# Smaller first layer-norm groups, an earlier modulation weight, 2 KB value runs and a new instruction order in a one-core adaLN transformer block

## The chip, the cores and the metric

The kernel runs on one core of a Trainium2 chip. The metric is the device time of one execution in microseconds (us), as the median of several executions. The profile lists the core's instructions by engine (in the kernel before 2264 matmuls on PE, 301 instructions on DVE, 189 on ACT, 81 on POOL): TensorE (PE, with its weight loads as PEld), VectorE (DVE), ScalarE (ACT), GpSimd (POOL) and SyncE (SP). In this kernel SP does nothing but issue DMAs, in a fixed order, each behind the semaphores that it waits for.

## The reference

One transformer block on x of 2048 tokens by 512, bf16, with a modulation from a condition vector c. Cut to what matters:

```python
mod = silu(c) @ w_mod                      # 6 vectors of 512: sa, ca, ga, sb, cb, gb
h = layernorm(x) * (1 + ca) + sa
q, k, v = h @ wqkv                         # 32 heads of 16
# each position attends to 8 keys: itself and those 2, 4, ... 14 positions before
attn = softmax(mask(q . k * 16**-0.5))
x = x + ga * ((attn . v) @ wo)
h = layernorm(x) * (1 + cb) + sb
x = x + gb * ((silu(h @ w1) * (h @ w3)) @ w2)      # w1, w3: 512 x 1792
```

w_mod is 512 x 3072. The kernel loads it in four parts: the first slice of 1 MB holds sa and ca, the second slice of 1 MB holds sb and cb, and two parts of 0.5 MB hold the gates ga and gb.

## The kernel before

x is cut into 16 tiles of 128 tokens. For a group of tiles the kernel normalizes (xn), transposes on TensorE, and applies the modulation while it evicts the result (h, by ScalarE) from PSUM (pall in the profile, which all matmuls here write). Then come the projections q, k and v. The window attention runs as one big VectorE product per tile (pq = q times the eight shifted copies of k, 128x4096), reduced on TensorE; v goes to a DRAM scratch and comes back in another layout (vsh), is multiplied with the weights by a second 128x4096 product and reduced on TensorE.

The program lists its operations with a number for each; a list scheduler at build time picks, for each engine, the ready operation with the lowest number, using modelled costs. So the order of instructions, the DMA order on SP included, comes from a table of numbers that was tuned offline, from the modelled DMA rate and from the pools of buffers.

```python
DMA_RATE = 320
BLOCKS = [[[0]], [[1]], [[2], [3]], [[4, 5], [6, 7]], ...]           # tiles whose exps are one block
LATE = {"wms1": 0, "wmg1": 1, "w13_0": 0, "w13_1": 1, ...}           # these loads wait for a pq product
...
p.dma(... c, transposed, elements of 2 bytes ..., ("load", 0), 1024, w=[vcT])
for T in range(4):
    p.dma(x_sb[:, T, :], x_view[:, T, :], ("load", 1), 131072, w=[vx[T]])
p.dma(wm_s[0][:], wm_view[:, :, 0:1024], ("load", 2), 1048576, w=[vwms[0]])      # first slice of w_mod
... wq, wk, wv, the other x, the first gate's weights, wo ...
late["wms1"] = [p.dma(wm_s[1][:], wm_view[:, :, 1536:2560], ("load", 12), 1048576, ...)]   # second slice
...
# one value tile back from the scratch: one DMA, runs of 8 rows = 8 KB
p.dma(lambda: vv.at[:].rearrange("p g d -> p (g d)"),
      bass.AP(v_dram, (PAD + T * P) * D, [[8 * D, 16], [-DIL * D, W], [1, 8 * D]]), ("vl", T), 1048576, ...)
...
for cch in range(NCH):                                   # four groups of four tiles
    vns = [ln_stats(0, 4 * cch + i) for i in range(4)]
    vh = ln_T(0, cch, vns)
    proj_qk(cch, 0, vh)
    proj_qk(cch, 1, vh)
    for i in range(4):
        proj_v(4 * cch + i, vh)
```

The softmax here doesn't subtract the row's maximum and nothing guards it: scores larger than these inputs give would overflow.

## Time and profile before

| | before |
|---|---|
| time, three runs at the start | 262.87 us (262.56 to 263.39) |
| profiled execution | span 259.8 us |
| TensorE busy | 242.0 us, 93% |
| VectorE busy | 191.5 us, 74% |
| first projection starts | 13.81 us |
| second slice of w_mod, issue to landing | 17.8 us |

From the profile's page: busy time of each engine, the busy tenths of TensorE and its granted clock in 40 slices of the span, the chain of work that ended last, and two of the DMA groups (count, size of each, median us from issue to landing).

```profile
span 259.8 us, 5381 instructions
PE 242.0 (93%) x2264; PEld 138.2 (53%) x2264; DVE 191.5 (74%) x301; ACT 109.1 (42%) x189; POOL 36.8 (14%) x81
...
PE   0489997699999999999999999999999999999995
...
PEclk9999999799999999999999999999999999999999
...
PE 83%; DMA 9%; DVE 4%; ACT 1%; POOL 1%; SPq 1%; issue 0%
...
sb_vsh<-v_scratch_dram SPq DMA_DIRECT2D x13, 1024.0 KB, 8.1
...
sb_wm_s<-in_w_mod_dram SPq DMA_DIRECT2D x2, 1024.0 KB, 11.9
```

The kernel is bound by TensorE: the chain lies on it for 83% of the span. A gain must come from its idle stretches, which are at slices 1 to 3 and at slices 7 and 8, or from the clock, which falls in slice 8 as well. The waits view of TensorE says what it waited for (total us, times, longest):

```profile
PE pall L574 <- DVE sb_xn L558: 6.6, 3, 6.0
PE pall L520 <- DMA sb_wm_s<-in_w_mod_dram: 4.9, 2, 3.7
PE pall L600 <- ACT sb_h L582: 3.1, 1, 3.1
PE pall L660 <- DVE sb_pq L651: 0.2, 1, 0.2
```

The timeline of TensorE shows where (start, us, engine, line, what, count, and in brackets the idle time before it and what ended it):

```profile
6.00 1.14 PE L574 MATMUL pall<-sb_ident,sb_xn 128*128 128x128 bf16 x8 [6.00 <-DVE sb_xn L558]
...
9.26 0.99 PE L520 MATMUL pall<-sb_csT_bf,sb_wm_s 128*128 128x1 bf16 x32 [1.22 <-DMA sb_wm_s<-in_w_mod_dram]
...
13.81 6.07 PE L600 MATMUL pall<-sb_h,sb_wqkv 128*128 128x512 bf16 x20 [3.11 <-ACT sb_h L582]
...
47.59 0.98 PE L520 MATMUL pall<-sb_csT_bf,sb_wm_s 128*128 128x1 bf16 x32 [3.70 <-DMA sb_wm_s<-in_w_mod_dram]
48.43 1.87 PE L600 MATMUL pall<-sb_h,sb_wqkv 128*128 128x512 bf16 x4
...
50.52 2.22 PE L600 MATMUL pall<-sb_h,sb_wqkv 128*128 128x512 bf16 x8
```

There are two costs. At the start, TensorE waits for the first xn, for w_mod and then for four 512-wide evictions of h. At 47.59 us it waits for the second slice of w_mod; the four matmuls after that wait take 1.87 us, where four take 1.03 us elsewhere: the clock was at half speed. The records of the clock show half speed from 47.75 to 51.17 us. They begin only at 17.03 us, with full speed; that the clock was at half before is read from the matmuls, since 20 of them take 6.07 us at 13.81 us where eight take 1.89 us later.

Lastly, the DMA view of the window from 27 to 50 us (GB/s in 40 slices of the window, then two groups):

```profile
GB/s 228 52 82 315 383 383 385 363 347 376 392 185 214 228 214 271 228 199 228 256 228 185 214 271 228 164 178 199 239 338 381 385 367 358 353 347 345 353 373 371
...
sb_vsh<-v_scratch_dram SPq DMA_DIRECT2D x2, 1024.0 KB, 13.9
...
sb_wm_s<-in_w_mod_dram SPq DMA_DIRECT2D x1, 1024.0 KB, 17.8
```

The stretch at about 200 GB/s, from the twelfth figure on, is the two value tiles on their way back. They landed at 40.19 and 44.85 us, behind 1.5 MB of weights, and the slice at 47.45 us behind them.

### The profile page before, as it was taken

How to read it: one execution, taken by the hardware profiler on the slowest of the kernel's cores; microseconds unless marked ns; L12 is line 12 of the kernel's file. 1: busy time of each engine (PE TensorE's matmuls, PEld its weight loads, DVE VectorE, ACT ScalarE, POOL GpSimd, SP SyncE). 2: the span in 40 equal slices, each digit the busy share in tenths (PEclk: the TensorE clock that was granted, in tenths of full speed). 3: DMA queues.
4: the chain of work that ended last, by engine and by line, in shares of the span. 5: the costliest groups of instructions: out<-in, count | busy, mean ns of one | idle time of the engine just before them, and what ended most of it. 6: DMA issues, size and time to landing. Idle time of an engine off the chain costs nothing.

```text
span 259.8 us, 5381 instructions
## 1 busy us (share of the span) xinstructions
PE 242.0 (93%) x2264; PEld 138.2 (53%) x2264; DVE 191.5 (74%) x301; ACT 109.1 (42%) x189; POOL 36.8 (14%) x81
## 2 busy tenths in 40 slices
PE   0489997699999999999999999999999999999995
PEld 0235655356459865656555455455654444566662
DVE  5596999589899998999899869877957434333152
ACT  2347755178677321636474044342205334311210
POOL 6174034100430004000000300001322000000000
PEclk9999999799999999999999999999999999999999
DMA  5992899989989559930784943909200000001001
GB/s 156 361 334 64 260 246 256 357 215 346 241 182 183 136 126 235 213 76 3 182 185 101 222 99 77 191 23 238 67 23 20 1 3 0 20 23 40 20 20 40
DMA packets 38904, 36.27 MB, mean 140 GB/s; under 512 B 18640, under 2 KB 35808, under 8 KB 36832
## 3 DMA queue, kind: packets, MB, share of 16 engines
q1 hardware_dynamic: 38880, 35.94, 54.9%
q8 instruction: 17, 0.28, 0.5%
q14 instruction: 7, 0.06, 0.1%
HBM read 30.67 MB, written 5.26 MB: 138 GB/s over the span
## 4 chain that ended last, share of the span: by engine, by line
PE 83%; DMA 9%; DVE 4%; ACT 1%; POOL 1%; SPq 1%; issue 0%
PE pall L756 37%; PE pall L777 19%; DMA sb_wm_s<-in_w_mod_dram 9%; PE pall L600 8%; PE pall L740 5%; PE pall L727 5%; PE pall L660 3%; PE pall L620 3%; PE pall L574 2%; DVE sb_pq L651 2%; ACT sb_h L582 1%; POOL sb_rs L555 1%; SPq L133 1%; PE pall L520 1%; DVE sb_st L550 0%
## 5 line engine op out<-in xcount | busy, mean ns | idle before, releaser
L756 PE MATMUL pall<-sb_h,sb_w 128*128 128x512 bf16 (+1 forms) x560 | 101.0, 336 | 0.0
L756 PEld LDWEIGHTS pall<-sb_h,sb_w 128*128 128x128 bf16 x560 | 53.9, 98 | 41.3
L762 ACT ACTIVATE sb_sg<-pall 128x512 bf16<-128x512 f32 (+1 forms) x70 | 35.4, 512 | 69.1 <-PE pall L756 69.0
L765 DVE TENSOR_TENSOR sb_hh<-sb_sg,pall 128x512 bf16<-128x512 bf16 (+1 forms) x70 | 38.6, 577 | 25.4 <-PE pall L756 21.8
L777 PE MATMUL pall<-sb_w,sb_hh 128*128 128x512 bf16 x224 | 51.3, 379 | 0.0
L651 DVE TENSOR_TENSOR sb_pq<-sb_q,sb_kT 128x4096 bf16<-128x4096 bf16 x16 | 36.3, 2282 | 2.3 <-ACT sb_q L607 1.9
L553 POOL TENSOR_TENSOR sb_rs<-sb_mv,sb_cst 128x1 f32<-128x1 f32 x32 | 14.3, 446 | 160.3 <-DVE sb_mv L551 160.1
L600 PE MATMUL pall<-sb_h,sb_wqkv 128*128 128x512 bf16 x128 | 33.1, 404 | 3.1 <-ACT sb_h L582 3.1
L777 PEld LDWEIGHTS pall<-sb_w,sb_hh 128*128 128x128 bf16 x224 | 21.5, 98 | 23.1
L718 DVE TENSOR_TENSOR sb_vsh<-sb_vsh,sb_al 128x4096 bf16<-128x4096 bf16 x13 | 29.6, 2285 | 3.2 <-DMA sb_al<-a_scratch_dram 2.2
L582 ACT ACTIVATE sb_h<-pall,sb_modc 128x512 bf16<-128x512 bf16 (+1 forms) x36 | 23.8, 730 | 18.9 <-PE pall L574 13.8
L550 DVE BATCH_NORM_STATS2 sb_st<-sb_x 128x6 f32<-128x512 bf16 x32 | 21.7, 679 | 3.2 <-DMA sb_x<-in_A_x_dram 2.9
L783 DVE TENSOR_TENSOR sb_o<-pall,sb_x 128x512 bf16<-128x512 f32 x16 | 11.0, 690 | 17.4 <-PE pall L777 17.2
L600 PEld LDWEIGHTS pall<-sb_h,sb_wqkv 128*128 128x128 bf16 x128 | 12.5, 103 | 17.1 <-ACT sb_h L582 3.4
L555 POOL TENSOR_TENSOR sb_rs<-sb_rs,sb_cst 128x1 f32<-128x1 f32 x32 | 20.4, 637 | 2.5
L574 PE MATMUL pall<-sb_ident,sb_xn 128*128 128x128 bf16 x128 | 12.6, 233 | 6.6 <-DVE sb_xn L558 6.6
L733 ACT ACTIVATE sb_ot<-pall 128x512 bf16<-128x512 f32 x16 | 9.6, 598 | 21.8 <-PE pall L727 19.8
L660 PEld LDWEIGHTS pall<-sb_E,sb_pq 128*128 128x128 bf16 x512 | 15.0, 96 | 3.2 <-ACT sb_h L582 0.3
L740 PE MATMUL pall<-sb_wo,sb_ot 128*128 128x512 bf16 x64 | 15.9, 379 | 0.0
L620 PE MATMUL pall<-sb_wqkv,sb_h 128*128 128x512 bf16 x64 | 15.8, 379 | 0.0
L574 PEld LDWEIGHTS pall<-sb_ident,sb_xn 128*128 128x128 bf16 x128 | 9.2, 103 | 12.0 <-DVE sb_xn L558 7.9
L660 PE MATMUL pall<-sb_E,sb_pq 128*128 128x32 bf16 x512 | 15.3, 176 | 0.2 <-DVE sb_pq L651 0.2
(59 smaller groups left out, 156.9 us busy)
## 6 DMA issues: line engine op xcount, KB each, us to landing
sb_vsh<-v_scratch_dram SPq DMA_DIRECT2D x13, 1024.0 KB, 8.1
sb_vshx<-v_scratch_dram SPq DMA_DIRECT2D x3, 1024.0 KB, 7.1
sb_wm_s<-in_w_mod_dram SPq DMA_DIRECT2D x2, 1024.0 KB, 11.9
v_scratch_dram<-sb_v SPq DMA_DIRECT2D x16, 128.0 KB, 6.3
sb_w<-in_B_w_dram SPq DMA_DIRECT2D x4, 512.0 KB, 11.9
out_dram<-sb_o SPq DMA_DIRECT2D x16, 128.0 KB, 1.7
sb_w<-in_B_w_dram SPq DMA_DIRECT2D x1, 1792.0 KB, 8.8
sb_wqkv<-in_A_wqkv_dram SPq DMA_DIRECT2D x3, 512.0 KB, 8.7
```

What stands on the lines that cost most here:

```text
L574: ins = e.transpose(b[:, col:col + P], vns[tt].at[:, ft * P:(ft + 1) * P], ident[:])
L582: return e.activation(vh.at[:, ft, 0:n * P], b[:, j * 512:j * 512 + n * P], ACT.Identity, bias=modc[:, 8 * which + ft:8 * which + ft + 1], ...
L600: ins = e.matmul(bank(vp), wqkv[:, t, col:col + P], vh.at[:, t, :], start=(t == 0), stop=(t == KT - 1))
L620: ins = e.matmul(bank(vp), vh.at[:, t, tt * P:(tt + 1) * P], wqkv[:, t, 2 * D:3 * D], start=(t == 0), stop=(t == KT - 1))
L651: return e.tensor_tensor(vp.at[:], in0, in1, ALU.mult)
L660: ins = e.matmul(b[:, c0:c0 + H], vp.at[:, w, ft, :], E_sb[:, ft, :], start=(ft == 0), stop=(ft == KT - 1))
L718: return e.tensor_tensor(v_w, v_w, a_w, ALU.mult)
L740: ins = e.matmul(bank(vy), vt.at[:, ft, :], wo[:, ft, :], start=(ft == 0), stop=(ft == KT - 1))
L756: ins = e.matmul(bank(vp)[:, 0:n], wt[:, t, fi * P:(fi + 1) * P], vh.at[:, t, 0:n], start=(t == 0), stop=(t == KT - 1))
L762: p.op("act", lambda e: e.activation(vt.at[:, 0:n], bank(vgp)[:, 0:n], ACT.Silu), c_act(n), k, r=[vgp], w=[vt], table="silu")
L765: p.op("dve", lambda e: e.tensor_tensor(vh_.at[:, 0:n], vt.at[:, 0:n], bank(vup)[:, 0:n], ALU.mult), c_dve(n), k, r=[vt, vup], w=[vh_])
L777: ins = e.matmul(bank(vz), vhh[fi].at[:, tt * P:(tt + 1) * P], w2[:, fi, :], start=(fi == 0), stop=(fi == NF - 1))
```

## The change

The intent is to start TensorE's projections sooner, and to keep the second modulation from ever waiting. In parts:

1. The first two layer-norm groups have two tiles rather than four, so the first evictions of h are 256 wide, and half of them go to VectorE. c is loaded from ACT's queue; two x tiles go ahead of w_mod and two behind it.
2. The second slice of w_mod stands ahead of all FFN weights on SP.
3. A value tile comes back as four DMAs with runs of 2 KB, not as one with runs of 8 KB.
4. The exps are blocked per pair of tiles, and all the numbers are tuned anew, so the order of instructions differs on every engine.

```diff
-DMA_RATE = 320
+DMA_RATE = 350
-BLOCKS = [[[0]], [[1]], [[2], [3]], [[4, 5], [6, 7]], [[8, 9], [10, 11]], [[12, 13], [14, 15]]]
-LATE = {"wms1": 0, "wmg1": 1, "w13_0": 0, "w13_1": 1, "w13_2": 2, "w13_3": 3, "w2": 4}
+BLOCKS = [[[0]], [[1]], [[2, 3]], [[4, 5]], [[6, 7]], [[8, 9]], [[10, 11]], [[12, 13], [14, 15]]]
+VG = 2
+LN1 = [[0, 1], [2, 3], [4, 5, 6, 7], [8, 9, 10, 11], [12, 13, 14, 15]]
+LATE = {"wms1": 0, "wmg1": 2, "w13_0": 0, "w13_1": 1, "w13_2": 1, "w13_3": 2, "w2": 2}
@@ loads
-    p.dma(... c ..., ("load", 0), 1024, w=[vcT])
+    p.dma(... c ..., ("load", 0), 1024, w=[vcT], eng="act")
     for T in range(4):
-        p.dma(x_sb[:, T, :], x_view[:, T, :], ("load", 1), 131072, w=[vx[T]])
+        p.dma(x_sb[:, T, :], x_view[:, T, :], ("load", 1 if T < 2 else 19), 131072, w=[vx[T]])
@@ evictions of h
+                if half and not which and gi < 2:
+                    p.op("dve", ev_dve, c_dve(n * P), k, r=[vt, vmod[which]], part=[vh])
+                else:
+                    p.op("act", ev, c_act(n * P) + 150, k, r=[vt, vmod[which]], part=[vh])
@@ value tile
+        for g in range(0, 8, VG):
+            p.dma(lambda g=g: vv.at[:, g:g + VG, :].rearrange("p g d -> p (g d)"),
+                  bass.AP(v_dram, (PAD + T * P + g) * D, [[8 * D, 16], [-DIL * D, W], [1, VG * D]]), ("vl", T), VG * 131072, ...)
@@ groups
-    for cch in range(NCH):
-        vns = [ln_stats(0, 4 * cch + i) for i in range(4)]
+    for gi, Ts in enumerate(LN1):
+        vns = [ln_stats(0, T) for T in Ts]
... the tables of numbers, projections of n columns, and one small VectorE operation less per modulation: left out ...
```

## The prediction

> **What bounds the kernel now.** TensorE. The engine table has PE busy 242.0 of a 259.8 us span (93%), DVE 191.5 (74%). PE's warm durations (0.216 us for a 512-column matmul, 0.109 for 256, 0.79 per logits or value reduction) add up to about 237 us. In the timeline PE's first projection starts at 13.81 us, after waits for xn (6.0), w_mod's DMA (1.2) and h (3.1); one more wait, 3.70 us ending at 47.59, is for the second w_mod slice, which took 17.85 us to land behind FFN weights and V loads. After that PE never idles over 0.3 us until 256.8; the tail is 3.0 us. Half-speed matmuls cost about 1.6 us before 17.0 (20 projections in 6.07 us, not 4.3) and 1.7 us after the 3.7 us gap (granted clock 0.5 for 3.4 us)[...].
>
> **What the change does.**
> 1. Start. w_mod is issued third, at about 1.7 us instead of 3.13, and c's 2-byte descriptors, during which almost no data moved (about 1.3 us), leave SP's queue for ACT's. w_mod lands near 7 instead of 9.12. The first h needs two tiles; its four evictions are 256 wide, two on ACT, two on DVE: about 0.9 us instead of 2.79. First projection at about 10.0; with 0.2 us less PE work before it, **gain 3.6 us**.
> 2. Second w_mod slice. It goes ahead of all FFN weights; only V loads (2 MB) precede it. I estimate landing at 33-36 us; PE wants it at about 36. The wait and its half-speed window go: **gain 5.0 us**.
> 3. V loads. Today's 8 KB packets move 110-115 KB per 0.5 us, where 1 and 2 KB packets move 165-185. With 2 KB runs a load should take 3-4 us rather than 4.2-4.7. V loads are not on PE's chain; this protects step 2. Cost: 48 more issues of 0.55 us on SP, hidden.
> 4. Exp per pair: two more table loads (1.28 us each) on ACT, 42% busy: nothing. 256-column projections: PE time the same within 0.1 us.
> 5. **New cost:** PE's work comes 8-9 us earlier while DVE's keeps its size. Adding DVE durations in the new order leaves only 1-2 us of slack ahead of PE's reductions between 27 and 85 us, and the first attention reloads queue behind 3.5 MB of FFN weights. I charge **1.5 us** of small PE waits.
>
> **Sum.** 262.9 - 3.6 - 5.0 + 1.5 = 255.8; I say **255.6 us**, range 252.8 to 259.6. Nothing shortens PE's 237 us, so about 252.5 is the floor. Chances: faster by over 2% (under 257.6) 0.78, within 2% 0.19, slower 0.03.
>
> **What the profile would show.** Step 1: first projection at 9.5-10.8 us. Step 2: no PE wait for w_mod over 1 us, no 0.5 clock window after 20 us. Step 3: V loads faster per MB, no PE wait for them. Step 5: PE waits on DVE products between 27 and 85 us, 1-3 us in all; DVE over 95% busy there, its total within 2 us of 191.
>
> **What would make it wrong.** c's tiny descriptors beside x may delay x and w_mod, halving step 1. The q/k weights now come after v and x; past 13.5 us PE waits and cools again. If 2 KB V runs are no faster, or SP blocks behind a V store, the second slice is late again (up to 4 us back). If DVE cannot hold the tighter plan, PE waits of 3-5 us appear before 90 us: 258-259.

## The result, and the profile after

| | before | after |
|---|---|---|
| time, same rounds | 263.13 us (4 runs, 262.56 to 264.07) | 255.37 us (4 runs, 254.32 to 255.82) |
| ratio | | 0.9696, 95% interval 0.9651 to 0.9741 |
| profiled span | 259.8 us | 253.2 us |
| first projection starts | 13.81 us | 10.51 us |
| second slice lands | 47.45 us | 36.90 us |

A ratio here is the mean time of one kernel's fast runs over that of the other's of the same rounds, so it is not quite the ratio of the quoted medians. Later, on chip 12, the changed kernel was run again (label after_again): 255.08 us against 262.20, ratio 0.9719 (0.9686 to 0.9751). All outputs are right.

From the page of the changed kernel:

```profile
span 253.2 us, 5473 instructions
PE 239.0 (94%) x2262; PEld 140.4 (55%) x2296; DVE 191.7 (76%) x298; ACT 111.4 (44%) x198; POOL 32.0 (13%) x81
...
PE   0599989999999999999999999999999999999995
...
PEclk9999999999999999999999999999999999999999
...
PE 87%; DVE 5%; DMA 2%; POOL 2%; issue 1%; SPq 0%; ACT 0%; DVEq 0%
...
sb_vsh<-v_scratch_dram SPq DMA_DIRECT2D x48, 256.0 KB, 4.4
...
sb_wm_s<-in_w_mod_dram SPq DMA_DIRECT2D x2, 1024.0 KB, 6.6
```

DMA's share of the chain fell from 9% to 2%, and no slice of the clock is below 9. The waits of TensorE:

```profile
PE pall L574 <- DVE sb_xn L558: 6.4, 2, 5.6
PE pall L522 <- DMA sb_wm_s<-in_w_mod_dram: 1.5, 1, 1.5
PE pall L633 <- DVE sb_xn L558: 1.3, 1, 1.3
PE pall L633 <- ACT sb_q L622: 0.2, 1, 0.2
```

One wait for w_mod is left, the one at the start. Its timeline:

```profile
5.62 0.61 PE L574 MATMUL pall<-sb_ident,sb_xn 128*128 128x128 bf16 x4 [5.62 <-DVE sb_xn L558]
7.76 0.99 PE L522 MATMUL pall<-sb_csT_bf,sb_wm_s 128*128 128x1 bf16 x32 [1.54 <-DMA sb_wm_s<-in_w_mod_dram]
...
10.51 3.59 PE L633 MATMUL pall<-sb_wqkv,sb_h 128*128 128x512 bf16 x8 [1.30 <-DVE sb_xn L558]
...
37.56 0.29 PE L574 MATMUL pall<-sb_ident,sb_xn 128*128 128x128 bf16 x2 [0.75 <-DVE sb_xn L558]
...
39.34 0.94 PE L522 MATMUL pall<-sb_csT_bf,sb_wm_s 128*128 128x1 bf16 x32
```

The wait of 1.30 us at 10.51 is put down to xn, which came last by the semaphores, but it is the time of the evictions of h: two on ScalarE and two on VectorE, between 9.4 and 10.5 us. The second modulation at 39.34 has no wait before it at all. The eight matmuls at 10.51 take 3.59 us, nearly twice what eight take at full speed (1.89): TensorE starts its projections at half clock here as well, and the records show full clock only from 16.28 us.

The mean granted clock of every run (an average over the execution, in which the half speed of the start isn't counted) shows the late half-speed stretch without a profile. One stretch of 3.41 us at half speed is a loss of 1.7 us of 260, so it makes 0.993, and two make 0.987. Of the 31 runs of the kernel before made beside the experiments, 11 had 0.992 or 0.993 and 20 had 0.985 to 0.987; none had 1.0. All ten runs of the changed kernel had 1.0.

### The profile page after: what moved, and what is told of

Same layout as the page of the kernel before. It is cut to its first block, busy times and chain, and to the rows that moved or that the text cites. A ratio compares the mean times of both kernels' runs of the same rounds, so it can differ in the third digit from the quotient of the medians.

```text
span 253.2 us, 5473 instructions
## 1 busy us (share of the span) xinstructions
PE 239.0 (94%) x2262; PEld 140.4 (55%) x2296; DVE 191.7 (76%) x298; ACT 111.4 (44%) x198; POOL 32.0 (13%) x81
## 4 chain that ended last, share of the span: by engine, by line
PE 87%; DVE 5%; DMA 2%; POOL 2%; issue 1%; SPq 0%; ACT 0%; DVEq 0%
PE pall L771 36%; PE pall L792 19%; PE pall L615 9%; PE pall L755 5%; PE pall L742 5%; PE pall L633 5%; PE pall L673 4%; PE pall L574 2%; DMA sb_x<-in_A_x_dram 2%; POOL sb_rs L555 1%; DVE sb_xn L558 1%; DVE sb_st L550 1%; POOL sb_rs L553 1%; DVE sb_pq L664 1%; DVE sb_hh L780 1%
## 5 line engine op out<-in xcount | busy, mean ns | idle before, releaser
L771 PE MATMUL pall<-sb_h,sb_w 128*128 128x512 bf16 (+1 forms) x548 | 100.0, 336 | 0.7
L780 DVE TENSOR_TENSOR sb_hh<-sb_sg,pall 128x512 bf16<-128x512 bf16 (+1 forms) x70 | 39.5, 577 | 26.0 <-PE pall L771 23.8
L792 PE MATMUL pall<-sb_w,sb_hh 128*128 128x512 bf16 x216 | 49.7, 379 | 0.4
L615 PE MATMUL pall<-sb_h,sb_wqkv 128*128 128x512 bf16 (+1 forms) x155 | 31.9, 344 | 0.3
L582 ACT ACTIVATE sb_h<-pall,sb_modc 128x512 bf16<-128x512 bf16 (+1 forms) x36 | 23.1, 708 | 18.7 <-PE pall L574 13.1
L553 POOL TENSOR_TENSOR sb_rs<-sb_mv,sb_cst 128x1 f32<-128x1 f32 x32 | 8.8, 276 | 151.4 <-DVE sb_mv L551 148.4
L733 DVE TENSOR_TENSOR sb_vsh<-sb_vsh,sb_al 128x4096 bf16<-128x4096 bf16 x12 | 27.3, 2285 | 0.4 <-DMA sb_vsh<-v_scratch_dram 0.4
L615 PEld LDWEIGHTS pall<-sb_h,sb_wqkv 128*128 128x128 bf16 x160 | 15.1, 101 | 11.0 <-ACT sb_h L582 0.7
L633 PE MATMUL pall<-sb_wqkv,sb_h 128*128 128x512 bf16 x63 | 17.6, 411 | 1.5 <-DVE sb_xn L558 1.3
L574 PEld LDWEIGHTS pall<-sb_ident,sb_xn 128*128 128x128 bf16 x128 | 9.5, 101 | 10.6 <-DVE sb_xn L558 6.9
L755 PE MATMUL pall<-sb_wo,sb_ot 128*128 128x512 bf16 x58 | 15.0, 379 | 0.3
```

The source lines that it names most:

```text
L574: ins = e.transpose(b[:, col:col + P], vns[tt].at[:, ft * P:(ft + 1) * P], ident[:])
L615: ins = e.matmul(bank(vp)[:, 0:n], wqkv[:, t, col:col + P], vh.at[:, t, 0:n], start=(t == 0), stop=(t == KT - 1))
L633: ins = e.matmul(bank(vp), vh.at[:, t, tt * P:(tt + 1) * P], wqkv[:, t, 2 * D:3 * D], start=(t == 0), stop=(t == KT - 1))
L733: return e.tensor_tensor(v_w, v_w, a_w, ALU.mult)
L755: ins = e.matmul(bank(vy), vt.at[:, ft, :], wo[:, ft, :], start=(ft == 0), stop=(ft == KT - 1))
L771: ins = e.matmul(bank(vp)[:, 0:n], wt[:, t, fi * P:(fi + 1) * P], vh.at[:, t, 0:n], start=(t == 0), stop=(t == KT - 1))
```

## Where the time went, from the two traces

In the profiled executions, over the 6.6 us of span:

| TensorE, us | before | after | difference |
|---|---|---|---|
| waits before the first projection (6.00+0.29+1.22+3.11; 5.62+1.54+1.30) | 10.6 | 8.5 | -2.2 |
| lost to half clock at the start (half of the busy time until full clock, modulation left out: 5.5; 7.0) | 2.8 | 3.5 | +0.7 |
| wait for the second slice | 3.7 | 0 | -3.7 |
| lost to half clock after that wait (half of 2.7, modulation left out) | 1.4 | 0 | -1.4 |
| other waits of at least 0.2 us (0.24+0.28; 0.20+0.75) | 0.5 | 1.0 | +0.4 |
| sum | | | -6.2 |

The modulation's 32 one-column matmuls are left out of the half-clock rows because the clock hardly changes them: they took 0.99 us at half speed (9.26 us, before) and 0.94 us at full speed (39.34 us, after). The 0.4 us that the sum leaves over stays unassigned; idle times under 0.2 us are not counted, and some matmul records are missing (the page of the changed kernel counts 2262 matmuls and 2296 weight loads).

The profiled execution of before was one of its faster ones (261.81 us against a median of 263.13), with one late half-speed stretch.

## The experiments

The experiments keep the compiled order of one of the two kernels and change one thing. `_move` takes operations out of the scheduled list and puts them behind another; the order on the other engines stays, and the semaphores are worked out anew. The theory was: the gain is the earlier start plus the absent wait for the second slice with its half-speed stretch, and the rest of the change is worth little. The rivals: that the new order alone carries the gain, that the value loads carry part of it, that a wait taken away comes back elsewhere. Each ratio is to the kernel before, on the same chip in the same rounds; "against the change" compares with after_again's median of 255.08 us, measured in the first group of runs (after_again, a_warm, a_loads, a_slice on one chip); for the other groups, whose before was within 0.6 us of that group's, I compare ratios.

### after_again: the changed kernel as it is

> The changed kernel itself, for comparison with the variants of this call on the same chip. Expected ratio to before 0.968 to 0.972. Both theories expect the same. To look at: the time at which the matmuls of the start turn to full speed (16.28 us in the first profile).[...]

255.08 us (six runs, 254.11 to 255.81), 0.9719. First projection at 10.61 us, full clock from 16.37 us, second slice landed at 36.84 us: the trace of after repeats. Whether the time of full clock moves from execution to execution can't be told from this pair (16.28 and 16.37 us). a_slice and a_vg8 below start with the same order and show that it does: 14.12 and 15.07 us.

### a_slice: the second slice behind FFN weights again

The second slice is moved behind 1.75 MB of FFN weights on SP; the rest of the changed kernel stays.

```diff
+    w = _find(p, "load", 12)                                            # second slice
+    last = [o for o in p.placed if o.key in (("load", 14), ("load", 15), ("load", 16))]
+    _move(p, w, last[3])
```

> The changed kernel with the second w_mod slice queued behind 1.75 MB of FFN weights; only the order on the DMA queue changes. Theory (the earlier slice is worth its wait): it lands at about 42.5 to 43 us instead of 36.9, TensorE waits about 3 us at 39.3 us, and the total rises by 3 to 5 us (the upper figure if the gap also turns the clock down). Rival (the gain is in the new compute order, which hides this wait, or VectorE is the true limit by then): the total rises by less than 1 us.

263.63 us (four runs), 1.0054 (1.001 to 1.0097). This one DMA's place takes back the whole gain, 8.5 us, more than I expected. It doesn't follow that the slice is worth the whole gain, since the wait that it makes is about twice that of the kernel before (7.2 us against 3.7). In the waits of TensorE:

```profile
PE pall L522 <- DMA sb_wm_s<-in_w_mod_dram: 8.8, 2, 7.2
```

The slice landed at 45.58 us, later than the 42.5 to 43 expected: behind the FFN weights, for which SP itself has to wait, it was issued only at 36.55 us, where the changed kernel issues it at 29.71. TensorE waited 7.2 us for it, with half clock from 41.42 to 51.66 us; all four runs had a mean clock of 0.981 to 0.987. The sum nearly closes for the profiled executions: a wait of 7.2 us, 2.4 us lost to half clock (half of the 4.9 us of work between 45.71 and 51.66 us, the modulation left out), 0.6 us of waiting for a value product and 0.2 us of issue, less 1.1 us because full clock happened to come at 14.12 us at the start rather than at 16.28, make 9.3 us; the spans differ by 262.9 - 253.2 = 9.7 us. So this wait cost about its length and half of the half-speed work after it, and the new order doesn't carry the gain by itself.

### b_slice and b_slice2: only the second slice's place, in the kernel before

The mirror image: in the kernel before, put loads behind the slice. b_slice moved one pair of FFN weights and the second gate's weights; b_slice2 moved the pair alone.

```diff
+    w = _find(p, "load", 12)[0]
+    _move(p, _find(p, "load", 15) + _find(p, "load", 13), w)            # b_slice
+    _move(p, _find(p, "load", 15), _find(p, "load", 12)[0])             # b_slice2
```

> The kernel before with one move on its DMA queue: the second w_mod slice goes ahead of one pair of FFN weights and of the second gate's weights (1.5 MB); nothing else changes. Theory: it lands about 4.5 us earlier, the 3.70 us wait at 43.9 us and the half-speed window after it go, and the total falls by 3.5 to 5.4 us (ratio 0.980 to 0.987). Rival (VectorE would hold TensorE back there anyway): the wait moves to another product and the total falls by less than 1.5 us.

265.97 us, 1.0122 (1.0088 to 1.0157): slower. This was a mistake of design, not a test of the theory: TensorE's order has the second gate ahead of the second modulation, the gate's weights now landed at 47.85 us, and TensorE waited 7.4 us for them:

```profile
PE pall L539 <- DMA sb_wm_g<-in_w_mod_dram: 7.4, 1, 7.4
```

> The kernel before with one pair of FFN weights (1 MB, which nothing waits for early) moved behind the second w_mod slice on the DMA queue; unlike b_slice the second gate's weights stay in front. Theory: the slice lands about 3 us earlier, at about 44.5 us, the 3.70 us wait shrinks under 1 us, the half-speed window after it goes, and the total falls by 3 to 5 us (ratio 0.981 to 0.989). Rival: another wait takes its place, total falls by less than 1.5 us.

263.38 us, 1.0047 (1.0016 to 1.0078): no gain, so the theory's number missed and the rival held. The slice landed at 45.06 us, and the wait for it fell from 3.70 to 0.36 us, as meant. But the FFN weights that now stood behind the slice came in front of the store of the first attention weights, which landed at 51.61 us, 8.8 us after its issue and 1.2 us later than in the kernel before (50.43 us), while TensorE was ready for what follows the exp at 50.6 us rather than 52.6; the buffers of the exps are freed by it, so ScalarE's exp waited, and TensorE waited for the exp. From the waits of that kernel, ScalarE's first and then two of TensorE's:

```profile
ACT sb_ex L674 <- DMA a_scratch_dram<-sb_attn: 3.6, 1, 3.6
...
PE pall L660 <- ACT sb_ex L674: 1.7, 1, 1.7
...
PE pall L520 <- DMA sb_wm_s<-in_w_mod_dram: 0.4, 1, 0.4
```

And half clock came twice, from 46.49 to 49.90 and from 53.32 to 56.73 us, although before the first of these TensorE had only waits of 0.24 and 0.36 us: it was busy 2.74 of the 3.41 us up to 46.49, mostly with matmuls of 32 columns and of one column. Whether such small matmuls have a part in the fall of the clock, no run here isolates. So in the kernel before neither move mended the slice's place alone: what stepped back on the queue was waited for itself (7.4 us for the gate's weights in b_slice) or delayed something else (the store, by 1.2 us, in b_slice2). In the changed kernel the value loads and the slice are earlier as a whole, and no wait of TensorE for the later FFN weights is in its list. The theory of step 2 therefore stands on a_slice and on the next run, not on this pair.

### b_vg2 and a_vg8: only the runs of the value loads

In the kernel before, each value load becomes four DMAs of 2 KB runs under one semaphore (so the number of DMAs changes with the runs); in the changed kernel VG goes from 2 to 8, which makes it one DMA of 8 KB runs again.

```diff
# b_vg2, in the kernel before
-        p.dma(... one load, [[8 * D, 16], [-DIL * D, W], [1, 8 * D]] ...)
+            for g in range(0, 8, 2):
+                ins = e.dma_start(vv.at[:, g:g + 2, :].rearrange("p g d -> p (g d)"),
+                                  bass.AP(v_dram, (PAD + T * P + g) * D, [[8 * D, 16], [-DIL * D, W], [1, 2 * D]]))
# a_vg8, in the changed kernel
-VG = 2
+VG = 8
```

> The kernel before with each V load as four DMAs of 2 KB runs; nothing else changes. Theory (V loads run a tenth faster and matter only through what queues behind them): the first two land about 0.8 us earlier together, the second w_mod slice too, the wait of 3.70 us shrinks to about 3 us, and the total falls by 0.5 to 2.5 us (more than the wait if the shorter gap no longer turns the clock down). Rival (the re-layout is a main source of the gain): it falls by over 3 us.

260.83 us, 0.9911 (0.9859 to 0.9963), within the theory's 0.5 to 2.5 us. The value loads, still behind the same weights, landed at 42.64 us rather than 44.85, the slice at 45.19 rather than 47.45, and the wait fell from 3.70 to 1.23 us. The DMA view of 27 to 50 us shows why, beside the one of before:

```profile
GB/s 158 75 89 251 379 379 388 372 346 345 369 253 274 299 310 278 296 317 271 281 289 292 278 296 246 285 331 399 378 360 349 349 353 342 364 373 372 346 356 340
...
sb_vsh<-v_scratch_dram SPq DMA_DIRECT2D x8, 256.0 KB, 7.8
...
sb_wm_s<-in_w_mod_dram SPq DMA_DIRECT2D x1, 1024.0 KB, 11.5
```

Where 8 KB runs moved 164 to 271 GB/s, 2 KB runs moved 246 to 331. Worked out from landings, a value tile of 1 MB took 5.3 us before (34.18 to 44.85 us for two) and 4.1 us here (34.46 to 42.64). The four runs were 258.21 us at a mean clock of 1.0 (the profiled one, so the wait of 1.23 us is that of the fastest), 261.00 and 260.66 at 0.993, and 261.93 at 0.987: with the 2 KB runs, the clock shows a late half-speed stretch in three of the four executions and none in the fourth.

> The changed kernel with each V load as one DMA of 8 KB runs, as before; the order on the compute engines is the same. Theory: loads take 4.2 to 4.7 us per MB instead of 4.0, the second w_mod slice lands at 37.5 to 38.5 us, still before TensorE wants it at 39.3, and the total stays within 0.6 us. Rival (the re-layout is a main source): it rises by over 2 us.

257.54 us, 0.9816 (0.9764 to 0.9867), about 2.5 us above the changed kernel, where I had expected at most 0.6. The two value loads landed at 28.63 and 33.75 us (5.1 us apart). In the profiled execution the slice was still in time, at 36.86 us, and TensorE instead waited 1.8 us at 175.6 us for a value product whose load was late:

```profile
PE pall L742 <- DVE sb_vsh L733: 1.8, 1, 1.8
```

This wait isn't that of the 8 KB runs alone: the profiled executions of a_slice, a_loads and a_four, with 2 KB runs, have it too (0.6, 0.8 and 1.2 us), those of after, after_again and a_evict don't. The four runs fall in two pairs: 256.43 and 256.22 us at a clock of 0.999 to 1.0, and 259.00 and 258.65 at 0.992 to 0.993. The second pair has the clock of one late half-speed stretch. A wait stood ahead of such a stretch in before (3.7 us) and in a_slice (7.2 us), so I suspect a long one here too, perhaps for the slice, though in b_slice2 waits of 0.24 and 0.36 us were all that stood ahead of one; those executions were not profiled, so which wait it was, if any, stays open. The rival's "over 2 us" holds here: the form of the value loads is worth about 1 to 2.5 us by itself, in both kernels. The changed kernel itself was measured on another chip, and the intervals are wide.

### a_loads, a_evict, a_four: the parts of the start

a_loads puts c back on SP's queue and all four x tiles ahead of w_mod. a_evict gives VectorE's evictions of the first two groups to ScalarE. a_four lets the first group's evictions wait for the fourth tile's xn, as a group of four would, with VectorE's statistics of tiles 2 and 3 moved ahead.

```diff
# a_loads
+    cT.eng = "sp"
+    _move(p, _find(p, "load", 19) + [cT], x1)
# a_evict
+        if o.key in (("tr", 1), ("tr", 3)) and o.eng == "dve":
+            o.eng = "act"
+            o.fn = o.alt
# a_four
+    _move(p, ops, p.placed[first - 1])            # statistics and xn of tiles 2 and 3
+    for o in ev:
+        o.deps[_find(p, "nm", 3)[0]] = True
```

> The changed kernel with the loads of the start issued as before: four x tiles, then c on SP's queue, then w_mod; the order on all compute engines is the same. Theory (w_mod's landing sets the start): w_mod lands at about 9.1 us instead of 7.6, the first projection moves from 10.5 to about 12.0 us, and the total rises by about 1.5 us (1.0 to 2.0). Rival (the two-tile groups alone bring the earlier start, the load order nothing): the total stays within 0.4 us.

256.41 us, 0.9773 (0.9742 to 0.9804): 1.3 us slower than the change, as expected. w_mod landed at 9.36 us, not 7.63, and the first projection came at 12.21 us:

```profile
12.21 3.59 PE L633 MATMUL pall<-sb_wqkv,sb_h 128*128 128x512 bf16 x8 [1.27 <-DVE sb_xn L558]
```

c's move to another queue didn't speed up the x tile beside it: with c on ACT's queue, where its load took 2.9 us to land, the second x tile took 3.0 us to land rather than 2.1. That the two loads slowed each other is my inference. This run doesn't separate c's move from the two x tiles' move.

> The changed kernel with all evictions of the first two normalised groups on ScalarE, as before; the order is else the same. Theory (the start is a chain of w_mod, modulation, eviction, projection): four evictions of 0.51 us in a row instead of two, the first projection at about 11.5 instead of 10.5 us, total up by 0.6 to 1.3 us. Rival: something else is late at that point (weights), total within 0.3 us.

256.61 us, 0.9770 (0.9742 to 0.9798), about 1.3 us slower than the change by the ratios, at the upper edge of the expected 0.6 to 1.3. The first projection came at 11.35 us, and the second group's h cost another wait of 0.8 us at 20.16.

> The changed kernel with the evictions of the first two-tile group made to wait until tiles 2 and 3 are normalised too, as a group of four must; VectorE's work for those tiles is moved ahead of its evictions, all else stays. Theory (the two-tile group takes x2 and x3 off the path to the first projection): xn of tile 3 at about 10.9 us, first projection at 11.8 to 12.3 instead of 10.5 us, total up by 0.5 to 1.6 us. Rival (w_mod is the true limit and the grouping is worth nothing): total within 0.3 us.

259.48 us, 0.9894 (0.9859 to 0.9929): about 4.5 us slower than the change. I had expected a first projection at 11.8 to 12.3 us and 0.5 to 1.6 us of loss. It came at 14.71 us:

```profile
14.71 3.59 PE L633 MATMUL pall<-sb_wqkv,sb_h 128*128 128x512 bf16 x8 [5.60 <-ACT sb_h L582]
```

The xn of tile 3 began only at 13.19 us. My edit had put the statistics and the xn of the two tiles one after the other, so VectorE waited for GpSimd's reciprocal deviation twice, 0.94 us each time; a good order of four would overlap these, so 4.5 us is an upper bound for the worth of the small groups. VectorE's work on the two tiles is 2 x (0.69 + 0.18 + 0.41) = 2.6 us even without the waits, so I estimate that the small groups are still the largest part of the start. The three losses don't add up to one number, since each moves the same first projection. Nor are they of the start alone: TensorE's late wait for a value product, told under a_vg8, is 0.8 us in a_loads and 1.2 us in a_four.

### a_warm, a_warm2 and a_best: is the half clock of the start worth anything?

The ledger above loses 3.5 us to half clock at the start of the changed kernel. Dummy matmuls on the identity, in TensorE's idle time before the first projection, were to bring the clock up sooner. a_warm issues 36, 14 and 12 matmuls of 128 columns; a_warm2 issues 9, 5 and 4 of 512 columns. a_best is a_warm2 with the scaling of wo (1.22 us of VectorE) moved behind the sixth pq product.

```diff
+        def fn(e):
+            for _ in range(n):
+                ins = e.matmul(p.pall[:, bank * 512:bank * 512 + 512], p.ident[:], eye4, start=True, stop=True)
+    warm(pe[0], 9, 0, ...)                                  # ahead of the first transposes
+    warm(_find(p, "mod", 2, "pe")[0], 5, 1)                 # ahead of the first modulation
+    warm([o for o in pe if o.key[0] == "v"][0], 4, 2)       # ahead of the first projection
+    _move(p, _find(p, "mod", 6), pq[5])                     # a_best only
```

> The changed kernel with 62 matmuls of the identity, whose results nobody reads, put into TensorE's idle time before the first projection; nothing else moves. Theory (the half clock after idleness costs about 2.6 us between 10.5 and 16.3 us): the projections run at 0.216 us from the first one, the 8 of 512 columns for V take about 1.7 us instead of 3.59, and the total falls by 1.0 to 2.6 us against the changed kernel, the rest going to waits for weights or VectorE. Rival (the early matmuls are slow because operands or evictions hold them up): they stay at 0.43 us and the total stays within 0.4 us, or rises.

255.37 us, 0.9731 (0.9702 to 0.9760): nothing gained. The clock was full from 5.55 us, and seven matmuls took 1.67 us at 10.77 us. But new waits took it back; from the waits of TensorE:

```profile
PE pall L615 <- DMA sb_wqkv<-in_A_wqkv_dram: 1.5, 2, 1.0
PE pall L574 <- DVE sb_xn L558: 1.4, 3, 0.8
```

Of the second, 0.75 us is in the changed kernel too. The third projection weight landed at 15.59 us rather than 14.33 us. In the trace one instruction fetch, a packet of 16,384 bytes that took 1.15 us, came at 12.2 us rather than 21.1 us, amid these loads. I infer that the 62 added matmuls and their weight loads brought it forward and that it held up the weight; with 18 added matmuls (a_warm2, below) the weight landed as in the changed kernel.

> As a_warm, but with 18 dummy matmuls of 512 columns instead of 62 of 128. In a_warm the added instructions brought an instruction fetch of 16 KB on one DMA engine forward from 21.1 to 12.2 us, and the weights and x tiles behind it landed 1.3 to 2.5 us late. Theory: the fetch moves back behind 18 us, the third weight lands at about 14.4 us again, the early waits of TensorE for weights fall from 1.5 to about 0.5 us; but VectorE's chain to the xn needed at 37.6 us hardly shortens, so TensorE waits there for 1.5 to 2.5 us instead of 0.75, and the total gains only 0.3 to 1.2 us on the changed kernel (ratio 0.967 to 0.971). Rival (the fetch was the only thing that cost a_warm its gain): total 2 us or more under the changed kernel (ratio under 0.965).

With 18 dummies the fetch came at 20.7 us and the weight at 14.35 us. 254.49 us (six runs, 253.45 to 255.20), 0.9703 (0.9674 to 0.9733). By the ratios that is 0.4 us below the changed kernel, and the intervals overlap, so it isn't shown to be faster. In the profiled execution the second modulation ran at 37.88 us rather than 39.34 us: of the 2.9 us of half clock in the projections, half was already gone there, 0.5 us of it to a wait for weights and 0.2 us to a first projection at 10.73 rather than 10.51 us. The wait of 0.82 us for an xn ahead of it is nearly the 0.75 us of the changed kernel.

> a_warm2, and the scaling of wo (1.22 us on VectorE, at 22.6 us, not needed before about 57 us) moved behind the sixth logits product. Theory (VectorE's chain to 37.6 us is the next limit after the half clock): the xn wait near 37 us shrinks by up to 1.2 us and the total is 1.0 to 2.5 us under the changed kernel (ratio 0.962 to 0.968). Rival (something other than VectorE holds TensorE there): no more than a_warm2 gives, within 0.3 us.

254.29 us (253.99 to 254.87), 0.9703 (0.9675 to 0.9731): no more than a_warm2. The VectorE work moved away from the xn came back as a wait of 1.0 us for a pq product at 52.52 us, as the rival had it. This is the lowest median measured, 3.0% below the kernel before, but it is not shown to differ from the changed kernel.

## Why the prediction was right

The prediction was 255.6 us, and 255.37 us was measured. The mechanism held; three of its terms had wrong sizes that cancelled, so the agreement to 0.2 us is luck.

- **Step 1, the start: direction right, size too large.** First projection expected at about 10.0 and within 9.5 to 10.8 us, measured 10.51. But "gain 3.6 us" took the whole advance for saved time, and that is the step that failed. Of the 3.3 us by which the first projection moved, 2.2 us are waits that went; the other 1.1 us are eight transposes that stood before it and now run after it. In the profiled executions 0.7 us more was lost to half clock, which nets 1.5 us: the projections ran at half clock until 16.28 us, 5.8 us after the first of them, where before it was 3.2 us (13.81 to 17.03). But this 0.7 us is the draw of two executions: without dummy matmuls, the delays from the first projection to full clock in the profiled executions lie between 3.2 and 5.8 us (3.5 us in a_slice, which starts in the order of the changed kernel). What sets the moment is not shown; the complete records of the clock in the two traces last 3.413 us (the late half-speed stretch of before) or 9, 61 and 70 times that (30.72 and 208.21 us in before, 238.93 us in after). Over before, b_slice, b_slice2 and b_vg2, which start alike, the delay averages 4.2 us and the half-clock loss at the start 3.3 us; over after, after_again, a_slice and a_vg8, 4.8 us and 3.0 us. So no lasting price of half clock is shown, and the start is worth 1.5 us in the profiled pair and about 2.4 us by these averages. Taken one by one, the loads and the eviction split were each worth about 1.3 us (a_loads, a_evict), the groups of two tiles up to 4.5 us (a_four).
- **Step 2, the second slice: right.** Expected to land at 33 to 36 us, it landed at 36.90, still ahead of the 39.34 us at which TensorE wanted it. The wait and the half-speed stretch are both gone: 3.7 + 1.4 = 5.1 us against "5.0". a_slice shows that the change can't do without it: with the slice late the gain is gone entirely (by a wait twice as long as that of before). By the mean clock (0.985 to 0.987 in 20 of 31 runs), it fell for two such stretches in most executions of before, which the profiled one doesn't show and the prediction doesn't count.
- **Step 3, the value loads: right in rate, wrong in worth.** "3 to 4 us" per MB was expected, and about 4.1 us was measured; but "V loads are not on PE's chain; this protects step 2" gave it no worth of its own. b_vg2 gained about 2 us by it alone (0.9911) and a_vg8 lost about 2.5 us. In the kernel before, the value loads stood in front of the slice that TensorE waited for, so they were on its chain through the queue.
- **Step 4, exps per pair: right.** ScalarE's busy time went from 109.1 to 111.4 us, and TensorE waited for no exp in the changed kernel.
- **Step 5, new waits: too large, and named the wrong operand.** 1.5 us of waits on VectorE's products was charged. Waits of at least 0.2 us came to 0.95 us in all, 0.4 us more than before, and the largest (0.75 us) was for an xn, not for a product. That xn waited for GpSimd (0.71 us of VectorE's time, ended by the reciprocal deviation): GpSimd's one-column addition, which takes 0.19 to 0.34 us elsewhere in this trace, took 2.14 us when it began at 34.28 us, just after a pq product of 2.26 us had begun on VectorE at 34.12. The addition ended at 36.42 us, with the product (36.38). The kernel before has two such additions of 2.14 us as well, begun 0.16 us after a product and ended with it (38.57 and 45.83 us, the products at 38.53 and 45.79). I infer from these times that the product held the addition up; by what means, the traces don't show. VectorE was busy 54.77 of the 58 us from 27 to 85 us, 94%, just under the 95% expected; its total changed by 0.2 us.

From the windows view, the stretch from 27 to 85 us; first the kernel before (busy us and count of each engine, mean clock, DMA share, GB/s):

```profile
27.00:85.00 58.00, 53.78 (x655) 33.42 (x652) 51.10 (x71) 37.17 (x68) 11.16 (x8) 0.97 0.98 255
```

and then the changed kernel:

```profile
27.00:85.00 58.00, 56.71 (x670) 36.48 (x678) 54.77 (x72) 37.74 (x71) 7.92 (x10) 1.00 0.88 254
```

The two engines gained busy time together, 2.9 us on TensorE and 3.7 us on VectorE, which fits the wait of 3.7 us taken away from both. So VectorE doesn't look like the new limit there, only close to it.

What remains open: which wait the two longer runs of a_vg8 had; how much of the gain at the start is the loads', the eviction split's and the groups' each; what the new instruction order is worth apart from the loads, which no run isolates; what sets the moment at which the clock turns; and why two thirds of the executions of before have a second half-speed stretch, since the profiled one had only one.

## What to carry to other kernels

When one DMA queue feeds everything, ask of each load who waits for what stands behind it: a transfer that no engine waits for is on the chain if it holds up one that is (here the value loads: 0.9911 for b_vg2), and moving a load back may delay a store that frees a buffer (b_slice2: 1.2 us). Price an idle gap on TensorE with the half-speed stretch after it where the trace shows one (here 1.4 us after a wait of 3.7 us, none after one of 1.23 us in b_vg2), and count for an earlier start only the waits that go, not the work that changes its place. After a wait is removed, look for the engine next in line (here VectorE, at 94%) before expecting more from the same place.
